# Sparse attention with a MoE projection: TensorE transposes for the first keys and queries, whole w_out tiles, and a planner that models a shared port

## The chip, the cores and the metric

The kernel runs on one core of one Trainium2 chip. The metric is the device time of one execution in microseconds, the median of several runs. Engines are named as in the profile: PE is TensorE (PEld its weight loads), DVE is VectorE, ACT is ScalarE, POOL is GpSimd, SP is SyncE, which here only issues DMAs. PSUM is the accumulator memory that PE writes, SBUF the working memory.

## The reference

Four batches of eight heads, 768 positions, head size 64. Scores are masked by blocks of 32: a block pair is kept if it is within one of the diagonal, in the first or last block row or column, or among three sampled blocks per row. The softmax times v, gathered over heads, gives x (3072 tokens by 512). A two-layer projection with a per-unit leaky slope follows.

```python
scores = scale * np.matmul(q, k.transpose(0, 1, 3, 2))
mask = np.abs(blk_i - blk_j) <= window          # or first/last block, or sampled
scores = np.where(mask, scores, -1000000000.0)
attn = softmax(scores)                          # max, exp, sum + 1e-9
x = (attn @ v).transpose(0, 2, 1, 3).reshape(B * S, H * D)
h = x @ w_in                                    # 512 -> 2048
g = np.maximum(h, 0.0) + alpha * np.minimum(h, 0.0)
out = g @ w_out                                 # 2048 -> 512
```

## The kernel before

**Precision.** All inputs are f32. Each matmul operand is split into two f16 tiles, a high half and a low half (value times a power of two, minus the high half), and products are summed from three or four such terms. High halves are made in `times` (L325 on ACT, L327 on DVE, L329 on POOL), low halves in `rest` (L333 on DVE in one two-input instruction, or L335 and L336 on POOL in a multiply and a subtraction).

**Attention.** Twelve chunks: each batch has three chunks of two 128-row query tiles. A unit is one chunk and one pair of heads (48 units), a step is one head's query tile in a unit (192 steps, 16 a chunk). A step is: scores on PE (L498, high and low query halves in one 128-deep operand against the key tile `kt` and against `ks`, which is `kt` with its two 64-partition halves swapped), bias and minimum on DVE (L508), exp with row sum on ACT (L515), a scale (L519) and reciprocal (L523), high and low half of the probabilities `ph`, one DMA transpose of `ph` into `pt` on SP's queue (L538). After the four steps of a unit PE multiplies by v (`av`, L552), and ACT and DVE write the two halves of `x` (L563, L568).

**Keys and queries.** `prep_k` loads two heads of keys, takes a sum of squares on ACT, a norm through PE and a scale on DVE, makes `kn` with both halves, transposes it by DMA into `kt` (`emit_k_t`, L444) and copies that by two DMAs into `ks` (`emit_k_swap`, issued in the helper `load`, L364). `prep_q` does the same for queries and transposes `qn` into `qt` (`emit_q_t`, L410). All these DMAs are issued on SP's queue.

**Weights.** w_in tiles (16, each 128x1024 int32 words as loaded) are staged in the memory of `wo`; w_out tiles are loaded as two halves of 128x512 words, one in a buffer of the tag `vf` (shared with the raw keys and values), one in a buffer of the tag `g` (shared with the MoE's activations). Three integer operations turn the words into scaled f32: n1 (L708, DVE), n2 (L713 on ACT or L715 on DVE), n3 (L720, DVE). Then come a sum of squares, a scale, and high and low halves. For w_in the low half comes from PE (L776, L777, copied by L781).

**MoE.** For each chunk, eight groups j of two 128-wide slices of the hidden layer: up projection on PE (L852), activation on DVE (L862, L863), high half on ACT (L868), low half on POOL (L873), down projection on PE (L891). The first up projection of a chunk needs the chunk's four `x`; the first down projection needs w_out's halves, whose scale needs all 16 w_out tiles.

**The planner.** The class `Plan` decides the order of all work and, where there is a choice (`alts`), the engine. Every operation has a priority in units of attention steps, a cost per engine, dependences and buffers that it takes and frees. `Plan.run` simulates the engines in time with these costs and starts, whenever an engine is free, the ready operation of lowest priority number. The order that comes out is fixed for each engine: on the chip each engine runs its list in that order and waits where an input is late. Two costs for DVE stand for POOL idle and POOL busy:

```python
MOE_LAG = 11.753          # steps between a chunk's last step and its MoE
MAX4 = {"DVE": (0.55, 1.1), "ACT": 0.85}     # a 128x768 high half
LOW4 = {"DVE": (0.94, 1.5), "POOL": 2.8}     # a 128x768 low half
```

`V_WI + W_WI * f` and `V_WO + W_WO * f` are the priorities of weight tile f. The pools `o` and `s` are two PSUM buffers each, `a` and `h` one each.

Of the kernel before, what the change touches and what calls it, by code (L numbers as in the profile page):

```python
# [54 lines left out]
class Plan:  # L55
# [5 lines left out]
    LAT = {"PE": 0.15, "DVE": 0.11, "ACT": 0.12, "POOL": 0.08}  # L61
# [4 lines left out]
    def buf(self, pool):  # L66
        return Buf(pool)
# [105 lines left out]
def attn_moe(ctx: ExitStack, tc: tile.TileContext, q, k, v, sampled, w_in, w_out, alpha, out):  # L173
# [100 lines left out]
    bias = cpool.tile([P, NT, S], BF16, name="bias")  # L274
    nident = cpool.tile([P, P], F16, name="nident")
# [64 lines left out]
    MAX4 = {"DVE": (0.55, 1.1), "ACT": 0.85}  # L340
    LOW4 = {"DVE": (0.94, 1.5), "POOL": 2.8}
# [668 lines left out]
```

## Time and profile before

| | us |
|---|---|
| median of 3 runs | 908.3 (907.07 to 909.03) |
| the profiled execution | 911.63 |
| its span | 909.9 |
| PE busy | 802.7 (88%) |
| DVE busy | 714.8 (79%) |
| ACT busy | 553.3 (61%) |
| POOL busy | 505.2 (56%) |
| mean granted TensorE clock | 0.955 |

Busy times are sums of instructions over the span. The page also cuts the span into 40 slices of 22.7 us and gives the busy share of each in tenths. A group of instructions has one line: its place in the kernel, engine, operation, output and inputs by name, count, busy time, mean in ns, and the idle time of its engine just before, with what ended most of that. A minimum, median and maximum stand in the view by tile or line. The stretches that the prediction shows list the busy time of each engine in a part of the span, the granted clock (1 is full speed) and the share of time in which the 16 DMA engines were busy, which can come out a little above 1.

### The profile page before, as it was taken

The page shows a single profiled execution, that of the slowest core. Times are in us where ns is not written, and L with a number is a line of the kernel's source. Part 1 is how long each engine was busy: PE and PEld are TensorE (multiplying, and loading weights), DVE is VectorE, ACT ScalarE, POOL GpSimd, SP SyncE. Part 2 cuts the span into 40 slices and gives each one's busy share as a digit, 9 for nine tenths or more (in the row PEclk, how much of TensorE's full clock was granted, in tenths as well). Part 3 has the DMA queues.
Part 4 walks back from the last instruction along what each step waited for, and adds up shares of the span by engine and source line. Part 5 has one row for each costly group of instructions (what it writes and reads, how often), then busy time and mean ns, then how long its engine had stood idle before and what let it go on. Part 6 is the DMA issues. An engine that isn't in the chain of part 4 may idle for free.

```text
span 909.9 us, 16946 instructions
## 1 busy us (share of the span) xinstructions
PE 802.7 (88%) x6089; PEld 528.9 (58%) x6089; DVE 714.8 (79%) x1468; ACT 553.3 (61%) x1185; POOL 505.2 (56%) x413
## 2 busy tenths in 40 slices
PE   3757438988888999999989999999989999999998
PEld 1323215646555766666656766566656667666664
DVE  4899999997888898879987877688987887765232
ACT  6697667875755756757566565666566556664111
POOL 3154445775656667566576665456567566555221
PEclk9867767999999999999999999999999999999999
DMA  9997986988997876969976868969976868655000
GB/s 264 288 263 180 203 210 117 185 134 136 170 175 133 156 138 129 210 130 189 202 154 128 128 128 150 189 119 193 187 140 118 156 117 139 116 117 105 1 24 23
DMA packets 393236, 137.45 MB, mean 151 GB/s; under 512 B 355236, under 2 KB 383936, under 8 KB 393152
## 3 DMA queue, kind: packets, MB, share of 16 engines
q1 hardware_dynamic: 354816, 94.41, 60.2%
q10 hardware_dynamic: 38272, 41.95, 16.8%
q8 instruction: 47, 0.77, 0.3%
q14 instruction: 37, 0.30, 0.1%
q0 software_dynamic: 64, 0.02, 0.0%
HBM read 35.67 MB, written 6.29 MB: 46 GB/s over the span
## 4 chain that ended last, share of the span: by engine, by line
DVE 33%; PE 29%; issue 13%; ACT 12%; DMA 5%; POOL 4%; ACTq 2%; POOLq 0%; DVEq 0%
PE h L852 11%; PE o L891 10%; DVE e L508 6%; ACT e L515 5%; PE sp L498 4%; DVE g L862 4%; DVE ph L333 3%; PE av L552 3%; DVE ph L327 3%; ACT ph L325 2%; DVE g L863 2%; ACTq L364 2%; DMA kf<-in_k_dram 2%; DVE wo L720 2%; DVE qn L403 2%
## 5 line engine op out<-in xcount | busy, mean ns | idle before, releaser
L852 PE MATMUL h<-x,wi 128*128 128x256 f16 x2304 | 270.3, 274 | 14.9 <-DVE g L863 14.7
L852 PEld LDWEIGHTS <-wi 128*128 128x128 f16 x2304 | 227.1, 99 | 57.0 <-issue 18.4
L515 ACT ACTIVATE e<-e,nm 128x768 f32<-128x768 f32 x192 | 178.6, 930 | 114.4 <-DVE nm L508 106.7
L891 PE MATMUL o<-wo,gh 128*128 128x512 f16 x768 | 230.8, 382 | 0.0
L336 POOL TENSOR_TENSOR ph<-e,ph 128x768 f16<-128x768 f32 x128 | 216.7, 1693 | 10.7
L873 POOL TENSOR_TENSOR gl<-g,gh 128x512 f16<-128x512 f32 x96 | 119.1, 1241 | 177.8 <-ACT gh L868 173.4
L335 POOL TENSOR_SCALAR e<-e,rs 128x768 f32<-128x768 f32 x128 | 130.2, 1017 | 157.3 <-DVE ph L327 81.2
L508 DVE CUSTOM_DVE_ANT_0 e<-sp,bias,cs 128x768 f32<-128x768 f32 x192 | 191.9, 1008 | 17.0 <-PE sp L498 10.2
L891 PE MATMUL o<-wo,gl 128*128 128x512 f16 x384 | 146.4, 381 | 1.8 <-POOL gl L873 1.8
L868 ACT CAST gh<-g 128x512 f16<-128x512 f32 x96 | 59.1, 616 | 135.4 <-DVE g L863 120.1
L498 PE MATMUL sp<-kt,qt 128*128 128x512 f16 (+1 forms) x384 | 99.1, 341 | 46.7 <-DVE nm L508 46.5
L498 PEld LDWEIGHTS <-qt 128*128 128x128 f16 x768 | 74.4, 101 | 111.3 <-issue 58.4
L325 ACT ACTIVATE ph<-e,rs 128x768 f16<-128x768 f32 x114 | 105.8, 928 | 28.1 <-DVE rs L523 21.5
L891 PEld LDWEIGHTS <-gh 128*128 128x128 f16 x768 | 74.9, 99 | 80.0 <-issue 3.4
L862 DVE TENSOR_SCALAR g<-h,am 128x256 f32<-128x256 f32 x192 | 83.2, 474 | 48.3 <-PE h L852 46.7
L552 PE MATMUL av<-pt,v 128*64 128x256 f16 x1728 | 108.0, 281 | 1.8 <-DMA pt<-ph 1.5
L552 PEld LDWEIGHTS <-v 128*64 128x64 f16 x1728 | 93.6, 113 | 18.8 <-issue 14.7
L498 PE MATMUL sp<-ks,qt 128*128 128x512 f16 (+1 forms) x384 | 99.3, 342 | 0.0
L523 DVE RECIPROCAL rs<-dn 128x1 f32<-128x1 f32 x192 | 29.0, 156 | 76.0 <-ACT dn L519 75.1
L333 DVE SCALAR_TENSOR_TENSOR ph<-e,rs,ph 128x768 f16<-128x768 f32 x64 | 75.2, 1175 | 9.9 <-ACT ph L325 8.6
L863 DVE SCALAR_TENSOR_TENSOR g<-h,gsc,g 128x512 f32<-128x512 f32 x96 | 72.1, 751 | 3.4
L891 PEld LDWEIGHTS <-gl 128*128 128x128 f16 x384 | 37.8, 99 | 49.4 <-POOL gl L873 3.8
(119 smaller groups left out, 734.1 us busy)
## 6 DMA issues: line engine op xcount, KB each, us to landing
wo<-in_moe_w_in_dram ACTq DMA_DIRECT2D x16, 512.0 KB, 6.7
raw<-in_moe_w_out_dram ACTq DMA_DIRECT2D x32, 256.0 KB, 3.8
kf<-in_k_dram ACTq DMA_DIRECT2D x16, 384.0 KB, 4.1
qf<-in_q_dram ACTq DMA_DIRECT2D x48, 128.0 KB, 4.1
ks<-kt SPq DMA_DIRECT2D x32, 192.0 KB, 4.3
vf<-in_v_dram ACTq DMA_DIRECT2D x16, 384.0 KB, 7.6
out_dram<-ob ACTq DMA_DIRECT2D x24, 256.0 KB, 3.5
pt<-ph SPq DMA_TRANSPOSE x192, 4.1
```

The lines of the kernel that those rows point to most:

```text
L325: nc.scalar.activation(dst, src, AF.Copy, scale=scale)
L333: nc.vector.scalar_tensor_tensor(dst, src, scale, hi, ALU.mult, ALU.subtract)
L335: nc.gpsimd.tensor_scalar(tmp, src, scale, 1.0, ALU.mult, ALU.mult)
L336: nc.gpsimd.tensor_tensor(dst, tmp, hi, ALU.subtract)
L498: nc.tensor.matmul(T["sp", n][:, a:z], T["qt", u][:, h, i, :], kt[:, h, a:z], start=(x == 0), stop=(x == 1))
L508: nc.vector.tensor_tensor_reduce(T["e", n], T["sp", n], bias[:, t0 + j % w, :], scale=T["cs", c][:, hp : hp + 1], scalar=3.0e38, op0=ALU.a ...
L515: nc.scalar.activation(T["e", n], T["e", n], AF.Exp, bias=T["nm", n], scale=-1.0, accum_out=T["su", n])
L552: nc.tensor.matmul(av[h * D : (h + 1) * D, : n * P], v2[:, h, t, vv, :], T["pt", u, h][:, pl * NT + t, :], start=(m == 0), stop=(m == len( ...
L852: nc.tensor.matmul(ph[:, i, :], win(w, f, ct), x[:, ct, :], start=(m == 0), stop=(m == len(terms) - 1))
L862: nc.vector.tensor_scalar(g[:, i, :], ph[:, i, :], 0.0, am1[:, f : f + 1], ALU.min, ALU.mult)
L873: nc.gpsimd.tensor_tensor(T["gl", c, j], T["g", c, j], T["gh", c, j], ALU.subtract)
L891: nc.tensor.matmul(T["o", c][t], g[:, i, t * P : (t + 1) * P], wout(w, f), start=(f == 0 and m == 0), stop=(f == NF - 1 and m == 2),)
```

## The change

There are four parts. First, for batch 0 the key tiles `kt` and `ks`, and for chunk 0 the query tiles `qt`, are no longer transposed by DMA: PE transposes the f16 halves into a PSUM buffer of the pool `o` (128x128 blocks for `kt` and `qt`; 128x64 blocks written to the opposite partition half for `ks`, so that no swap copy is needed), and ACT or DVE copies the result to SBUF. Second, w_out tiles are loaded whole (128x1024 words) into two new buffers `wr` or into the two buffers of `x`, the MoE's input, whichever is free. Third, the planner's cost model: latencies and a slack factor per engine are larger, DMAs are 15% longer, and operations whose cost is a pair take part in a port: a DVE operation with a pair starts only when no POOL operation is in its locked part (the second number of POOL's pair), and a POOL operation with no unlocked part waits for DVE. POOL may now also make the 128x768 high halves. Fourth, buffer counts and the priority constants are new. The path for probabilities by PE (`P_PE`, `emit_p_pe`, `emit_p_copy`) is written but off, since `P_PE` is 0.

```diff
-MOE_LAG = 11.753
-MOE_BOOST = 7.325
-V_WI = -10.661
-W_WI = 1.102
-V_WO = 12.217
-W_WO = 1.038
+MOE_LAG = 7.669
+MOE_BOOST = 7.439
+V_WI = -2.266
+W_WI = 0.799
+V_WO = -2.974
+W_WO = 1.152
...
-PL_V = -12.594
-P_V = -6.546
+PL_V = -35.527
+P_V = 5.696
-LD = 4
+LD = 5
+P_PE = 0
+RAWP = ["wr", "x"]
+K_PE = 1
+BUFS = {"wr": 2, "vf": 4, "qf": 4, "qt": 3, "qn": 2, "ph": 4, "e": 4, "pt": 4, "x": 2, "g": 3, "junk": 2, "sid": 2, "kt": 4, "ks": 4, "v2": 4, "gh": 3, "gl": 3}
...
-    LAT = {"PE": 0.15, "DVE": 0.11, "ACT": 0.12, "POOL": 0.08}
+    LAT = {"PE": 0.2, "DVE": 0.2, "ACT": 0.2, "POOL": 0.15}
+    SLACK = {"PE": 1.0, "DVE": 1.08, "ACT": 1.05, "POOL": 1.1, "SP": 1.0}
...
         def cost(o, e):
             c = o.alts[e]
-            if isinstance(c, tuple):
-                c = c[1] if idle["POOL"] > now + 0.2 else c[0]
-            return c
+            return self.SLACK[e] * (sum(c) if isinstance(c, tuple) else c)
+
+        def hold(o, e):
+            c = o.alts[e]
+            if not isinstance(c, tuple):
+                return 0.0
+            if e == "DVE":
+                return max(port["to"] - now, 0.0) if port["from"] <= now else 0.0
+            return max(port["dve"] - now, 0.0) if c[0] == 0 else 0.0
...
-                    best = min(o.alts, key=lambda e: max(idle[e] - now, 0.0) + load[e] + cost(o, e))
+                    best = min(o.alts, key=lambda e: max(idle[e] - now, hold(o, e)) + load[e] + cost(o, e))
+                    if hold(o, best) > 1e-9:
+                        continue
...
+                    if isinstance(o.alts[best], tuple):
+                        if best == "DVE":
+                            port["dve"] = now + c
+                        else:
+                            port["from"], port["to"] = now + self.SLACK[best] * o.alts[best][0], now + c
...
-                    rings["SP" if o.eng == "SP" else "ACT"].append([o.dma, o])
+                    rings["SP" if o.eng == "SP" else "ACT"].append([1.15 * o.dma, o])
...
-    bufs = dict(kt=5, ks=5, v2=5, vf=5, qf=6, qt=3, qn=2, ph=4, e=3, pt=3, x=2, g=3, gh=3, gl=3, junk=2, sid=2)
+    bufs = dict(BUFS)
...
-    MAX4 = {"DVE": (0.55, 1.1), "ACT": 0.85}
-    LOW4 = {"DVE": (0.94, 1.5), "POOL": 2.8}
+    MAX4 = {"DVE": (0.55, 0), "ACT": 0.85, "POOL": 1.05}
+    LOW4 = {"DVE": (0.94, 0), "POOL": (1.05, 1.65)}
...
+    def emit_k_pe(b, hp, x, h):
+        nat = T["kn", b, hp]
+        key = ("kt", "ks")[x]
+        if (key, b, hp) not in T:
+            T[key, b, hp] = wt(key, [P, 2, NT, P], F16)
+        t = T["kp", b, hp, x, h] = ps_o.tile([P, 2 * DM], F16, tag="o", name="kp")
+        for i in range(NT):
+            g = h * NT + i
+            if x == 0:
+                nc.tensor.transpose(t[:, i * P : (i + 1) * P], nat[:, g].rearrange("p a d -> p (a d)"), ident16)
+                continue
+            for a in range(2):
+                nc.tensor.transpose(t[D * (1 - a) : D * (2 - a), i * P : (i + 1) * P], nat[:, g, a, :], ident16)
...
+    def emit_q_pe(u):
+        n = chunks[units[u][0]][2]
+        T["qt", u] = wt("qt", [P, 2, n, P], F16)
+        T["qp", u] = ps_o.tile([P, 2 * DM], F16, tag="o", name="qp")
+        for g in range(2 * n):
+            nc.tensor.transpose(T["qp", u][:, g * P : (g + 1) * P], T["qn", u][:, g].rearrange("p a d -> p (a d)"), ident16)
...
+        if b == 0 and K_PE:
+            for x, d, kb in ((0, o_kt, kbuf), (1, o_ks, ksbuf)):
+                d[b, hp] = []
+                for h in range(2):
+                    tb = plan.buf("o")
+                    t = plan.op(prio - 2, {"PE": 0.4 + 0.4 * x}, lambda x=x, h=h: emit_k_pe(b, hp, x, h), [o], [tb, kb[b, hp]], [nb])
+                    d[b, hp].append(plan.op(prio - 2, {"ACT": 0.85, "DVE": 0.9}, lambda e, x=x, h=h: emit_k_copy(e, b, hp, x, h), [t], [kb[b, hp]], [tb]))
+            return
...
-        if h == 0:
-            t = wt("vf", [P, 512], I32, "raw")
-        else:
-            t = wt("g", [P, 512], I32, "raw")
-        load(e, t, wo_src[:, f, h * 512 : (h + 1) * 512])
+        t = wt(h.pool, [P, 1024], I32, "raw")
+        load(e, t, wo_src[:, f, :])
...
-        for h in range(2):
-            rb = plan.buf("vf" if h == 0 else "g")
-            o = plan.op(p - 8 + 0.1 * h, LQ, lambda e, f=f, h=h: emit_load_w(e, "wo", f, h), [n3wi[min(NF - 1, 8 + f // 2)]], [rb, plan.buf("ld")], dma=0.8)
-            o = plan.op(p, {"DVE": (0.22, 0.6)}, lambda f=f, h=h: emit_n1("wo", f, h), [o] + free, [], [rb])
-            o = plan.op(p, {"ACT": 0.7, "DVE": (0.34, 0.5)}, lambda e, f=f, h=h: emit_n2(e, "wo", f, h), [o], [], [rb])
-            n3.append(plan.op(p, {"DVE": (0.34, 0.5)}, lambda f=f, h=h: emit_n3("wo", f, h), [o], [], [rb]))
+        rb = plan.buf(*RAWP)
+        o = plan.op(p - 8, LQ, lambda e, f=f, rb=rb: emit_load_w(e, "wo", f, rb), [n3wi[min(NF - 1, 8 + f // 2)]], [rb, plan.buf("ld")], dma=1.6)
+        o = plan.op(p, {"DVE": (0.36, 0)}, lambda f=f: emit_n1("wo", f, 0), [o] + free, [], [rb])
+        o = plan.op(p, {"ACT": 1.27, "DVE": (0.6, 0)}, lambda e, f=f: emit_n2(e, "wo", f, 0), [o], [], [rb])
+        n3 = [plan.op(p, {"DVE": (0.61, 0)}, lambda f=f: emit_n3("wo", f, 0), [o], [], [rb])]
...
-                gl[j] = plan.op(p - MOE_BOOST, {"POOL": 0.2 + 1.1 * f}, lambda j=j: emit_gl(c, j), [o], [lbs[j]], [gb[j], hbs[j]])
+                gl[j] = plan.op(p - MOE_BOOST, {"POOL": (0, 0.1 + 1.08 * f)}, lambda j=j: emit_gl(c, j), [o], [lbs[j]], [gb[j], hbs[j]])
```

The copies of the transposed keys and queries (`emit_k_copy`, `emit_q_copy`) are one ACT or DVE copy of 128x768 or 128x512 f16 elements from PSUM.

More of the change, by code (lines that the diff above doesn't have):

```diff
@@ L93, in run @@
         order = []
+        port = {"from": 0.0, "to": 0.0, "dve": 0.0}
         busy = dict.fromkeys(self.ENGINES, 0.0)
@@ L133, in run @@
                     for b in o.alloc:
-                        self.free[b.pool] -= not b.live
+                        if not b.live:
+                            b.pool = next(x for x in b.pools if self.free[x] > 0)
+                            self.free[b.pool] -= 1
                         b.live = True
@@ L540, in emit_p_t, with emit_p_pe, emit_p_copy @@
         )
+    def emit_p_pe(n, x):
+        u, j = steps[n]
+        w = chunks[units[u][0]][2]
+        h, i = divmod(j, w)
+        if ("pt", u, h) not in T:
+            T["pt", u, h] = wt("pt", [P, 2 * NT, w * P], F16)
+        t = T["tp", n, x] = ps_o.tile([P, 2 * DM], F16, tag="o", name="tp")
+        for g in range(NT):
+            nc.tensor.transpose(t[:, g * P : (g + 1) * P], T["ph", n][:, x, g * P : (g + 1) * P], ident16)
+    def emit_p_copy(e, n, x):
+        u, j = steps[n]
+        w = chunks[units[u][0]][2]
+        h, i = divmod(j, w)
+        dst = T["pt", u, h][:, x * NT : (x + 1) * NT, i * P : (i + 1) * P]
+        src = T["tp", n, x][:, :S].rearrange("p (x j) -> p x j", j=P)
+        if e == "ACT":
+            nc.scalar.copy(dst, src)
+        else:
+            nc.vector.tensor_copy(dst, src)
     def emit_av(u):
@@ L663, in values @@
         p = first[u + 1] + 2
-        last = [o_pt[n] for n in range(first[u], first[u + 1])]
-        o = plan.op(p - 2, {"PE": 0.4 + 1.92 * f}, lambda: emit_av(u), last + [o_v2[b, hp]],
+        last = [x for n in range(first[u], first[u + 1]) for x in o_pt[n]]
+        o = plan.op(p - 2, {"PE": 0.3 + 1.88 * f}, lambda: emit_av(u), last + [o_v2[b, hp]],
                     [ab, xbuf[c]], [ptbuf[u, 0], ptbuf[u, 1], vbuf[b, hp]])
@@ L811, in attn_moe @@
             for x in (f - 1, f):
-                o = plan.op(p + 0.1, {"ACT": 0.63, "DVE": (0.36, 0.7), "POOL": 0.82}, lambda e, x=x: emit_w_hi(e, "wi", x), [gs[-1], prev])
+                o = plan.op(p + 0.1, {"ACT": 0.63, "DVE": (0.36, 0), "POOL": 0.82}, lambda e, x=x: emit_w_hi(e, "wi", x), [gs[-1], prev])
                 if WI_LO == "pe":
@@ L817, in attn_moe @@
                 else:
[L818 removed]
+                    prev = o_wi[x] = plan.op(p, {"DVE": (0.67, 0), "POOL": (0.8, 1.25)}, lambda e, x=x: emit_w_lo(e, "wi", x), [o], [], [sb])
     o_gsc = plan.op(V_WI + W_WI * NF - 2, {"DVE": 0.5}, emit_gsc, gs + [o_al])
```

73 lines of the change are left out of this document (49 added, 24 removed).

## The prediction

> **What bounds the kernel now.** I first read the page's busy shares and its forty slices.
>
> ```profile
> PE 802.7 (88%) x6089; PEld 528.9 (58%) x6089; DVE 714.8 (79%) x1468; ACT 553.3 (61%) x1185; POOL 505.2 (56%) x413
> PE   3757438988888999999989999999989999999998
> DVE  4899999997888898879987877688987887765232
> ```
>
> No single engine bounds the whole span. From slice 10 on PE is full; before it DVE is full and PE is not. So I cut the span where the first MoE product starts and asked for busy times by stretch, with two later stretches that hold a change of batch.
>
> ```profile
> 0.00:42.00 42.00, 21.46 (x56) 10.62 (x57) 28.62 (x85) 27.04 (x59) 10.73 (x27) 0.94 1.04 270
> 42.00:147.00 105.00, 58.59 (x292) 30.31 (x290) 96.97 (x214) 79.81 (x184) 49.87 (x39) 0.70 0.86 206
> 147.00:207.00 60.00, 55.56 (x424) 37.31 (x423) 58.89 (x113) 45.82 (x97) 42.59 (x33) 0.95 0.89 155
> 207.00:300.00 93.00, 80.69 (x650) 53.36 (x648) 75.86 (x151) 55.63 (x118) 56.82 (x46) 0.98 0.88 156
> 400.00:500.00 100.00, 94.54 (x738) 63.55 (x735) 85.54 (x177) 64.20 (x133) 61.26 (x48) 0.98 0.82 160
> 600.00:700.00 100.00, 92.22 (x728) 62.01 (x728) 85.06 (x173) 65.04 (x133) 62.85 (x48) 1.00 0.88 159
> ```
>
> After the stretch's length the columns are PE, PEld, DVE, ACT and POOL busy, granted clock, DMA share, GB/s. Up to 147 us PE works 21.46 + 58.59 = 80.0 us and DVE 28.62 + 96.97 = 125.6 us; DVE has 8.0 us of gaps in the 105 us of the second stretch. Behind 147 us PE works 802.7 - 80.0 = 722.7 us in the 762.9 us that are left, so it idles 40 us there, 12.3 + 5.5 + 7.8 = 25.6 us of it in the three stretches with a batch change. The end is therefore: the time until the first up projection may start, then 722.7 us of PE work, then 40 us of gaps. Most of the edits act on the first term, so the next view is what lets that projection start: two rows in order of time, and the rows of the w_out tiles with minimum, median and maximum in ns, and the first and last start.
>
> ```profile
> 146.79 3.46 PE L852 MATMUL h<-x,wi 128*128 128x256 f16 x16
> 147.48 0.41 DVE L568 SCALAR_TENSOR_TENSOR x<-av,x 128x256 f16<-128x256 f32 x1
> L720 DVE SCALAR_TENSOR_TENSOR wo<-raw,wo x32: 396/414/1871, 75.6 to 147.9; 128x256 int32<-128x256 int32 x32
> L708 DVE TENSOR_SCALAR wo<-raw x32: 269/280/1726, 74.0 to 142.1; 128x256 int32<-128x256 int32 x32
> L715 DVE SCALAR_TENSOR_TENSOR wo<-raw,wo x17: 403/412/1054, 74.4 to 146.7; 128x256 int32<-128x256 int32 x17
> ```
>
> The fourth x of chunk 0 ends within a microsecond of the first up projection, and the conversion of w_out ends with it (75.6 to 147.9): attention of chunk 0 and both weight conversions share DVE and finish together. What DVE has done by then, by line (busy us, mean ns):
>
> ```profile
> L720 DVE SCALAR_TENSOR_TENSOR wo<-raw,wo 128x256 int32<-128x256 int32 x31 | 23.0, 762 | 1.5 <-ACT raw L713 1.3
> L508 DVE CUSTOM_DVE_ANT_0 e<-sp,bias,cs 128x768 f32<-128x768 f32 x22 | 21.9, 1006 | 3.5 <-PE sp L498 3.5
> L720 DVE SCALAR_TENSOR_TENSOR wi<-wo,wi 128x512 int32<-128x512 int32 x16 | 12.5, 786 | 0.2 <-ACT wo L713 0.2
> L708 DVE TENSOR_SCALAR wo<-raw 128x256 int32<-128x256 int32 x32 | 11.1, 377 | 0.0
> L715 DVE SCALAR_TENSOR_TENSOR wi<-wo,wi 128x512 int32<-128x512 int32 x13 | 8.8, 679 | 0.1
> L715 DVE SCALAR_TENSOR_TENSOR wo<-raw,wo 128x256 int32<-128x256 int32 x17 | 8.0, 486 | 0.0
> L327 DVE TENSOR_SCALAR ph<-e,rs 128x768 f16<-128x768 f32 x8 | 7.6, 953 | 0.0
> L333 DVE SCALAR_TENSOR_TENSOR ph<-e,rs,ph 128x768 f16<-128x768 f32 x6 | 6.6, 1102 | 0.0
> L708 DVE TENSOR_SCALAR wi<-wo 128x512 int32<-128x512 int32 x16 | 6.6, 423 | 0.0
> L523 DVE RECIPROCAL rs<-dn 128x1 f32<-128x1 f32 x20 | 2.9, 153 | 2.7 <-ACT dn L519 2.6
> ```
>
> The means lie far above the medians of the view before (762 against 414 ns). The order of time shows why: a DVE instruction beside a two-input POOL subtraction lasts as long as that does.
>
> ```profile
> 99.13 1.76 POOL L336 TENSOR_TENSOR ph<-e,ph 128x768 f16<-128x768 f32 x1
> 99.31 1.73 DVE L708 TENSOR_SCALAR wo<-raw 128x256 int32<-128x256 int32 x1
> ```
>
> That is 1.73 us for work with a median of 0.28, while L508, which reads its scores from PSUM, keeps its 1.006 us.
>
> **The change, part by part.**
>
> *w_out tiles whole.* 32 half conversions become 16 whole ones. Now they cost 23.0 + 11.1 + 8.0 = 42.1 us of DVE by 147 us. The same three instructions on whole tiles stand in the w_in rows: 16 x 0.786 + 16 x 0.423 + 8.5 x 0.679 = 25.1 us (8.5 is half of 17, the share that DVE takes from ACT). That saves 17.0 us, if whole w_out tiles meet POOL as seldom as w_in's do. The other bound is merging alone, no stall avoided: 32 x 0.414 + 32 x 0.280 + 17 x 0.412 = 29.2 us by the medians, less 16 x 0.68 + 16 x 0.423 + 8.5 x 0.679 = 23.4 us whole (0.68 for L720 too, which has L715's shape): 5.8 us. I take the middle, **11.4 us**, since DVE meets POOL per instruction and there are half as many, but more attention will run beside them.
>
> *The plan knows the port.* It no longer starts such a DVE operation while POOL subtracts, and picks another. It also slows every cost by up to a tenth and lets POOL take the 128x768 high halves. What can go in the front, beside w_out: 8 x (0.953 - 0.62) = 2.7 us on L327, 0.62 being this line's median over the span (row below); 6 x 0.1 = 0.6 us on L333, if 1.0 is its undisturbed time; 16 x (0.786 - 0.68) = 1.7 us on L720 of w_in. So 0 to 5.0 us. The plan's times will drift from the chip's, so half: **2.5 us**.
>
> ```profile
> L327 DVE TENSOR_SCALAR ph<-e,rs x78: 600/620/1993, 55.3 to 827.7; 128x768 f16<-128x768 f32 x78
> 52.51 2.36 POOL L335 TENSOR_SCALAR e<-e,rs 128x768 f32<-128x768 f32 x1 [1.92 <-ACT ph L325]
> 50.03 4.15 DVE L333 SCALAR_TENSOR_TENSOR v<-vf,sv,v 128x768 f16<-128x768 f32 x4
> ```
>
> The lower two rows speak for the half: POOL's one-input multiply, which the new plan lets run beside DVE (its 1.05 of LOW4), took 2.36 us beside DVE's two-input operations. The Trainium skill ("SBUF — State Buffer", SBUF: two separate sides) says the same as a rule: the shared port pair is an exclusive lock for a whole instruction, against any GpSimd operation, so a plan that exempts L335 still has stalls in it. By that rule this term would be nearer 0 than 5.0, and the sum 2.5 us smaller.
>
> *Keys and queries by TensorE.* Gone are four key transposes, four query transposes and eight swap copies, all on SP's queue and in the first 60 us:
>
> ```profile
> 25.57 9.95 SPq L444 DMA_TRANSPOSE kt<-kn  x2
> 42.52 0.85 PE L498 MATMUL sp<-kt,qt 128*128 128x512 f16 x2
> q1 hardware_dynamic: 10496, 3.67, 32.1%
> kt<-kn SPq DMA_TRANSPOSE x4, 9.4
> L308 ACT ACTIVATE bias<-mkr 128x768 bf16<-128x768 f32 x6 | 4.6, 805 | 1.1 <-PE mkr L293 1.1
> L781 ACT CAST wi<-d 128x512 f16<-128x512 f32 x16 | 9.4, 587 | 4.0 <-PE d L777 4.0
> ```
>
> A key transpose takes 9.4 us to land here, its issue holds SP's queue, and the first score waits until 42.5 us. q1's 32.1% of 62 us is 20 us of all sixteen DMA engines at a time when they are full (share 1.04 up to 42 us), so the weight and value loads gain too. In its place: 4 x (12 + 24) + 16 = 160 PE transposes and 20 evictions. No row shows a transpose of this kind; between the mean weight load of the first stretch (10.62/57 = 0.19 us) and the mean score matmul (0.85/2 = 0.43 us, with two to four times the columns) they take 30 to 68 us of PE; I take 30, the narrower tile being nearer, all of it before the first up projection, where PE idles 147 - 80.0 = 67 us: nothing on the path. Without that gap it would be 30 us. The evictions read PSUM like L308 and L781: 16 x 0.805 + 4 x 0.587 = 15.2 us, on ACT, which idles 42 - 27.04 = 15.0 us in the first stretch. All of it on DVE would be some 19 us (16 x 1.006 + 4 x 0.7); none, 0. With ACT the cheaper and freer, a third on DVE: **5 us lost**. The scores can start near 20 us. DVE is the bound, so the 22 us are not won; what is won is DVE idleness, 13.4 us up to 42 us, of which 10.4 less 0.2 come before the first statistic (row below), plus 3.5 us waiting for scores (L508's row): 0 to 7, I take **4 us**.
>
> ```profile
> 10.41 0.15 DVE L313 TENSOR_SCALAR uq<-ssq 128x1 int32<-128x1 int32 x1 [3.74 <-ACT junk L321]
> ```
>
> *New constants.* w_out's conversion gets priorities -3 to 14 where it had 12 to 28, w_in's ends at 10, MOE_LAG falls from 11.8 to 7.7 steps. By the first up projection 22 steps had been scored where chunk 0 has 16; a step costs DVE 1.006 + 0.153 + (7.6 + 6.6)/20 = 1.87 us. Between 0 and 6 of them can come later (11.2 us); I take 3: **5.6 us** earlier. Their matmuls come later too: two pairs a step of 0.85 us each at the lower clock of the front, some 0.8 of that at full clock, 3 x 2 x 0.68 = **4.1 us** given back.
>
> *Buffers.* e and pt get a fourth tile each; kt, ks, v2 and vf lose their fifth, qf two. Behind 207 us PE waits for DVE, in all 22.9 us:
>
> ```profile
> PE h L852 <- DVE g L863: 13.5, 11, 2.5
> PE sp L498 <- DVE nm L508: 9.4, 10, 3.5
> ```
>
> A better order with more e and pt can take away up to 15 us; later key tiles can add as much. I take **6 us** off.
>
> *Sum.* 11.4 + 2.5 + 4 + 5.6 - 5 = 18.5 us earlier, less 4.1, plus 6: 20.4 us. The profiled execution's span of 909.9 becomes 889.5; its time lay 1.7 us above its span (911.6) and 3.3 above the median of the runs (908.3), so the forecast is 889.5 + 1.7 - 3.3 = **888 us**.
>
> **The rivals.**
>
> *More than the front.* Stalls are in every stretch: L327 has 78 instructions up to 1.99 us. If the new order also closes most of the 40 us behind 147 us (25 instead of 6) and the w_out term reaches 17, the gain is 20.4 + 19 + 5.6 = 45 us: 863. For it: DVE holds 85 of 100 us between 400 and 500, so stalls there can still reach PE. Against: PE is 92 to 96% busy in those stretches, so each has little left to give.
>
> *The front moves and nothing follows.* Evictions wholly on DVE (19 instead of 5) and only the 5.7 us of merging: 20.4 - 14 - 5.6 = 0.8, and -5.2 with no gain behind: 908 to 914. The change then does what it says and is hidden by the DVE bound. That the port bookkeeping does nothing is in here.
>
> *Slower: batch changes lose their cover.* With four key tiles the next batch's first can only be written when the last chunk's first unit has been scored, 12 steps before the batch ends. Of 192 steps 170 follow the first up projection, to 831 us, 4.0 us each (row below), so batches change near 251, 443 and 635 us and 12 steps are 48 us of notice, against a chain of load, square, scale, high, low, transpose and swap. MOE_LAG's cover falls from 11.8 x 4.0 = 47 to 31 us. For it: the three stretches with a batch change already hold 25.6 us of PE idleness.
>
> ```profile
> L508 DVE CUSTOM_DVE_ANT_0 e<-sp,bias,cs x192: 991/1008/1019, 44.0 to 831.2; 128x768 f32<-128x768 f32 x192
> 215.75 9.33 DMA kf<-in_k_dram
> ```
>
> Against: this load, a piece of that chain and of the chain of waits, is 9.3 us, far below 48. If it decides, from a delay of over 31 us on, 15 us more are lost at each of three changes: 45 - 20 = +25, some 933; at 10 us each, 918.
>
> **How the numbers follow.** The forecast has 0.58, more than the front 0.18, nothing follows 0.09, batch changes 0.15. Changes within 0.2% (2 us) can't be told from none. Of "nothing follows" 0.05 lies within that, 0.01 below and 0.03 above. Faster 0.77, same 0.05, slower 0.18. The forecast's own range, from its bounds short of all meeting at one end, is 872 to 904; the range out to the rivals is 860 to 914, which leaves out the far side of the batch changes and the tail of the second case.
>
> **What would show it.** Right: first score near 20 us; first up projection near 128 us instead of 146.8; w_out's L720 x16 at a mean under 0.85 us; ks and kt copies from SP only 24 and 12; PE idleness behind the first up projection at or below 40 us. Evictions mainly on ACT. Wrong: a first up projection at 145 us or later; DVE rows still twice their medians; PE waits growing in the stretches of the batch changes.

## The result, and the profile after

The changed kernel takes **878.3 us** (median of four runs, 876.9 to 880.1) beside 907.7 us of the kernel before on the same chip: a ratio of 0.968, 95% interval 0.965 to 0.971. 888 had been forecast, with a range of 860 to 914. The sign and the range held; the split of the gain did not, as the profile shows at once. First its page (in the changed kernel's line numbers L947 is the up projection, L986 the down projection, L558 the scores, L568 the bias, L358 and L359 POOL's low half, L356 DVE's low half, L350 and L352 the high half on DVE and POOL, and L805, L812 and L817 the three conversion steps n1, n2, n3 of the weights):

```profile
span 876.4 us, 17097 instructions
PE 802.7 (92%) x6249; PEld 533.7 (61%) x6249; DVE 672.0 (77%) x1395; ACT 554.9 (63%) x1188; POOL 560.4 (64%) x458
PE   3856476999999999999999999999999999999997
DVE  3889989999977778779877777788787787666322
```

PE's busy time is the same 802.7 us as before, with 160 instructions more; its idle time fell from 909.9 - 802.7 = 107.2 to 73.7 us. Where, is read from the stretches before and behind the first up projection, first of the changed kernel, then of the kernel before (columns as in the prediction: PE, PEld, DVE, ACT and POOL busy, clock, DMA share, GB/s):

```profile
0.00:152.20 152.20, 91.55 (x511) 48.46 (x512) 128.03 (x275) 107.61 (x240) 86.96 (x84) 0.78 0.77 194
152.20:876.40 724.20, 711.17 (x5740) 485.21 (x5738) 544.02 (x1121) 447.29 (x949) 473.44 (x375) 1.00 0.79 144
```

```profile
0.00:146.80 146.80, 79.85 (x346) 40.79 (x347) 125.39 (x299) 106.72 (x242) 60.60 (x66) 0.77 0.91 225
146.80:909.90 763.10, 722.81 (x5745) 488.13 (x5743) 589.40 (x1171) 446.57 (x944) 444.58 (x347) 0.99 0.75 137
```

The first up projection starts at 152.2 us, **5.4 us later** than before, not 18.5 earlier. Behind it PE's gaps shrank from 763.1 - 722.8 = 40.3 to 724.2 - 711.2 = **13.0 us**, and PE's own work there from 722.8 to 711.2 us. So 5.4 - 27.3 - 11.6 = -33.5 us of span: all of the gain, and more, lies behind the point that the prediction tried to move. (The profiled execution of the kernel before took 911.6 us, 3.9 above its median, so the two profiles lie 33.5 us apart where the medians lie 29.4 apart.) PE's two main waits for DVE in that part, first before and then after, shrank from 27.2 to 7.9 us:

```profile
PE h L852 <- DVE g L863: 14.7, 13, 2.5
PE sp L498 <- DVE nm L508: 12.5, 13, 3.5
```

```profile
PE h L947 <- DVE g L958: 7.3, 9, 2.1
PE sp L558 <- DVE nm L568: 0.6, 3, 0.2
```

Each row gives the total, the number of waits and the longest. The three stretches with a batch change, 87, 95 and 92% busy before, are full now:

```profile
207.00:300.00 93.00, 91.17 (x743) 62.54 (x740) 76.47 (x164) 57.81 (x123) 59.26 (x47) 1.00 0.88 165
400.00:500.00 100.00, 98.44 (x794) 67.04 (x793) 81.41 (x174) 68.80 (x143) 69.86 (x54) 1.00 0.90 167
600.00:700.00 100.00, 99.08 (x798) 67.46 (x797) 77.76 (x169) 68.65 (x149) 69.97 (x55) 1.00 0.90 168
```

DVE behind the first up projection fell from 589.4 to 544.0 us. The groups of the changed kernel that show how, and the parts that replaced others in the front:

```profile
L356 DVE SCALAR_TENSOR_TENSOR ph<-e,rs,ph 128x768 f16<-128x768 f32 x64 | 76.6, 1197 | 11.1 <-ACT ph L348 10.6
L350 DVE TENSOR_SCALAR ph<-e,rs 128x768 f16<-128x768 f32 x44 | 41.8, 950 | 3.5 <-DMA pt<-ph 2.8
L352 POOL TENSOR_SCALAR ph<-e,rs 128x768 f16<-128x768 f32 x38 | 45.1, 1186 | 30.5 <-DVE rs L583 21.7 <-DVE wi L817 4.6 <-DMA pt<-ph 2.5
L817 DVE SCALAR_TENSOR_TENSOR wo<-raw,wo 128x512 int32<-128x512 int32 x16 | 15.8, 988 | 0.0
L817 DVE SCALAR_TENSOR_TENSOR wi<-wo,wi 128x512 int32<-128x512 int32 x16 | 13.1, 817 | 0.8 <-ACT wo L810 0.8
L812 DVE SCALAR_TENSOR_TENSOR wo<-raw,wo 128x512 int32<-128x512 int32 x14 | 10.4, 744 | 0.0
L805 DVE TENSOR_SCALAR wo<-raw 128x512 int32<-128x512 int32 x16 | 9.5, 602 | 0.0
L805 DVE TENSOR_SCALAR wi<-wo 128x512 int32<-128x512 int32 x16 | 9.4, 599 | 0.0
L812 DVE SCALAR_TENSOR_TENSOR wi<-wo,wi 128x512 int32<-128x512 int32 x11 | 9.1, 832 | 0.0
L483 PE MATMUL kp<-ident,kn 128*64 128x128 f16 x96 | 5.3, 267 | 1.8 <-ACT kt L489 1.0 <-DVE kt L491 0.7
L480 PE MATMUL kp<-ident,kn 128*128 128x128 f16 x48 | 5.2, 272 | 3.7 <-DVE uq L336 2.5 <-ACT ks L489 0.7 <-DVE ks L491 0.5
L489 ACT COPY kt<-kp 128x768 f16<-128x768 f16 x5 | 4.0, 796 | 3.5 <-PE kp L480 2.8 <-DVE qt L506 0.5 <-issue 0.2
```

DVE's high halves of probabilities went from 78 to 44 instructions, 64.3 to 41.8 us; 38 are on POOL. It also made ten high halves of v before (12.0 us) and makes none now. The means of the two `ph` rows did not fall (1175 to 1197 ns, 827 to 950). The w_out conversion costs 15.8 + 10.4 + 9.5 = 35.7 us where it cost 42.1, but w_in's went up from 12.5 + 8.8 + 6.6 = 27.9 to 13.1 + 9.1 + 9.4 = 31.6 us.

### The profile page after: what moved, and what is told of

Same layout as the page of the kernel before. It is cut to its first block, busy times and chain, and to the rows that moved or that the text cites. A ratio compares the mean times of both kernels' runs of the same rounds, so it can differ in the third digit from the quotient of the medians.

```text
span 876.4 us, 17097 instructions
## 1 busy us (share of the span) xinstructions
PE 802.7 (92%) x6249; PEld 533.7 (61%) x6249; DVE 672.0 (77%) x1395; ACT 554.9 (63%) x1188; POOL 560.4 (64%) x458
## 3 DMA queue, kind: packets, MB, share of 16 engines
q10 hardware_dynamic: 35968, 41.95, 16.7%
## 4 chain that ended last, share of the span: by engine, by line
PE 63%; DVE 14%; issue 8%; POOL 6%; ACT 6%; ACTq 2%; DMA 1%; POOLq 0%; DVEq 0%
PE h L947 21%; PE o L986 21%; PE sp L558 10%; PE av L633 8%; DVE e L568 2%; ACT e L575 2%; POOL ph L359 2%; ACTq L387 2%; POOL gl L968 2%; DVE wo L817 1%; DVE g L957 1%; POOL e L358 1%; ACT ph L348 1%; DVE g L958 1%; DVE qn L426 1%
## 5 line engine op out<-in xcount | busy, mean ns | idle before, releaser
L947 PE MATMUL h<-x,wi 128*128 128x256 f16 x2304 | 267.2, 273 | 7.3 <-DVE g L958 7.3
L947 PEld LDWEIGHTS <-wi 128*128 128x128 f16 x2304 | 225.0, 98 | 47.9 <-issue 10.2
L986 PE MATMUL o<-wo,gh 128*128 128x512 f16 x768 | 228.5, 379 | 0.0
L359 POOL TENSOR_TENSOR ph<-e,ph 128x768 f16<-128x768 f32 x128 | 217.9, 1702 | 10.7
L568 DVE CUSTOM_DVE_ANT_0 e<-sp,bias,cs 128x768 f32<-128x768 f32 x192 | 192.0, 1007 | 26.2 <-PE sp L558 16.6
L358 POOL TENSOR_SCALAR e<-e,rs 128x768 f32<-128x768 f32 x128 | 132.0, 1032 | 110.4 <-ACT ph L348 60.4
L986 PE MATMUL o<-wo,gl 128*128 128x512 f16 x384 | 145.5, 379 | 0.6 <-POOL gl L968 0.6
L558 PEld LDWEIGHTS <-qt 128*128 128x128 f16 x768 | 74.2, 102 | 84.9 <-issue 32.1
L986 PEld LDWEIGHTS <-gh 128*128 128x128 f16 x768 | 74.7, 98 | 78.6 <-issue 0.8
L558 PE MATMUL sp<-kt,qt 128*128 128x512 f16 (+1 forms) x384 | 98.9, 341 | 21.6 <-DVE nm L568 19.4
L348 ACT ACTIVATE ph<-e,rs 128x768 f16<-128x768 f32 x110 | 101.6, 926 | 12.3 <-DVE rs L583 5.8
L633 PE MATMUL av<-pt,v 128*64 128x256 f16 x1728 | 105.9, 278 | 0.0
L558 PE MATMUL sp<-ks,qt 128*128 128x512 f16 (+1 forms) x384 | 98.4, 339 | 0.0
L356 DVE SCALAR_TENSOR_TENSOR ph<-e,rs,ph 128x768 f16<-128x768 f32 x64 | 76.6, 1197 | 11.1 <-ACT ph L348 10.6
L986 PEld LDWEIGHTS <-gl 128*128 128x128 f16 x384 | 37.6, 98 | 46.3 <-POOL gl L968 1.1
L352 POOL TENSOR_SCALAR ph<-e,rs 128x768 f16<-128x768 f32 x38 | 45.1, 1186 | 30.5 <-DVE rs L583 21.7
## 6 DMA issues: line engine op xcount, KB each, us to landing
qf<-in_q_dram ACTq DMA_DIRECT2D x48, 128.0 KB, 4.3
```

The lines of the kernel that those rows point to most:

```text
L348: nc.scalar.activation(dst, src, AF.Copy, scale=scale)
L358: nc.gpsimd.tensor_scalar(tmp, src, scale, 1.0, ALU.mult, ALU.mult)
L359: nc.gpsimd.tensor_tensor(dst, tmp, hi, ALU.subtract)
L558: nc.tensor.matmul(T["sp", n][:, a:z], T["qt", u][:, h, i, :], kt[:, h, a:z], start=(x == 0), stop=(x == 1))
L568: nc.vector.tensor_tensor_reduce(T["e", n], T["sp", n], bias[:, t0 + j % w, :], scale=T["cs", c][:, hp : hp + 1], scalar=3.0e38, op0=ALU.a ...
L633: nc.tensor.matmul(av[h * D : (h + 1) * D, : n * P], v2[:, h, t, vv, :], T["pt", u, h][:, pl * NT + t, :], start=(m == 0), stop=(m == len( ...
```

## The experiments

In most of them one part is undone in the changed kernel; in three a part is put into the kernel before. When the first up projection starts, DVE has done the scores of 22 or 23 steps, so its start can be compared between kernels; only e4 (20 steps) and e12 (21) start it with less attention done, and so look earlier than they are. The table gives the ratio to the kernel before on the same chip (95% interval), and from each profile the first up projection, PE's idle time ahead of it, and the gaps and PE's work behind it. The profile is one execution, up to 4 us from the median.

| kernel | us | ratio | first up | idle ahead | gaps behind | work behind |
|---|---|---|---|---|---|---|
| before | 907.7 | 1 | 146.8 | 67.0 | 40.3 | 722.8 |
| changed | 878.3 | 0.968 (0.965-0.971) | 152.2 | 60.7 | 13.0 | 711.2 |
| e1, keys by DMA | 892.3 | 0.985 (0.981-0.988) | 164.8 | 80.7 | 14.6 | 715.2 |
| e2, no port in the plan | 928.1 | 1.025 (1.022-1.028) | 168.9 | 72.0 | 35.9 | 722.2 |
| e3, three e and pt | 915.0 | 1.010 (1.007-1.014) | 153.9 | 63.9 | 35.6 | 723.8 |
| e4, w_out halves | 889.3 | 0.982 (0.979-0.985) | 149.6 | 60.1 | 21.4 | 718.3 |
| e5, MOE_LAG 7.9 | 878.4 | 0.969 (0.965-0.972) | 151.8 | 60.0 | 13.3 | 711.3 |
| e6, W_WI 0.82 | 884.2 | 0.975 (0.972-0.978) | 151.8 | 58.8 | 15.7 | 714.5 |
| e7, old constants | 889.1 | 0.979 (0.975-0.984) | 158.0 | 66.8 | 15.8 | 714.3 |
| e8, before + tiles | 917.8 | 1.012 (1.008-1.016) | 133.5 | 56.8 | 55.1 | 726.2 |
| e9, before + port plan | 908.2 | 1.000 (0.998-1.003) | 173.4 | 92.9 | 18.3 | 712.9 |
| e10, e9 + tiles | 895.7 | 0.987 (0.981-0.994) | 162.6 | 86.9 | 18.4 | 710.5 |
| e11, no high half on POOL | 880.9 | 0.969 (0.964-0.975) | 144.8 | 57.1 | 18.8 | 715.0 |
| e12, other constants | 883.1 | 0.972 (0.968-0.976) | 147.9 | 60.1 | 17.3 | 718.5 |

### e1: first keys and queries by DMA again

```diff
-K_PE = 1
+K_PE = 0
```

> The changed kernel (878.3 us) with the first keys and queries transposed by DMA again, all else as it is. The changed kernel's first up projection starts at 152.2 us, later than the 146.8 us of the kernel before, so the prediction's term (earlier first product) did not come. Theory A, the gain lies behind the first up projection (gaps 13.0 us there instead of 40.4): first scores move back from 24.5 to some 42 us, about 12.5 us of PE transposes and 4.7 us of DVE copies go away, the first up projection stays within 5 us of 152 and the time within 5 us of 878. Theory B, the early scores carry the gain: the first up projection moves to 165 us or later and the time to 890 or more.

```profile
0.00:164.80 164.80, 84.08 (x346) 42.49 (x347) 127.63 (x273) 106.28 (x235) 75.37 (x77) 0.77 0.85 198
164.80:894.60 729.80, 715.24 (x5744) 487.16 (x5742) 542.79 (x1119) 442.44 (x945) 472.39 (x374) 1.00 0.77 144
```

892.3 us, 14 us more than the changed kernel. Theory B was right for this part: the first up projection moves 12.6 us back, to 164.8 (165 or later had been named), and the gaps behind it hardly change (14.6 against 13.0). TensorE's transposes are worth their 14 us ahead of the first up projection, while DVE's work there is the same (127.6 against 128.0, with one step and the 4.7 us of copies fewer): it is its idle time, 37.2 against 24.2 us, that they take away.

### e2: the port taken out of the plan

```diff
         def hold(o, e):
-            c = o.alts[e]
-            if not isinstance(c, tuple):
+            if True:
                 return 0.0
```

> The changed kernel with the port taken out of the plan: no operation is held back for it, costs as in the changed kernel (slack, latencies), so DVE operations cost their undisturbed time whatever POOL does. Theory A, the port in the plan closes the gaps behind the first up projection: PE's gaps there grow from 13 to 25 us or more, the slow DVE rows (low halves, high halves) get longer means, time 890 or more. Rival, the plan's port moves stalls but saves none (w_in's conversion rows got slower in the changed kernel, 27.9 to 31.6 us): time within 5 us of 878.

```profile
168.90:927.00 758.10, 722.18 (x5740) 488.69 (x5738) 612.35 (x1165) 397.13 (x880) 472.63 (x369) 0.99 0.75 137
```

928.1 us, slower than the kernel before. Gaps behind the first up projection are 35.9 us, and that projection starts 16.7 us later. The groups of DVE show both ways in which the port acts:

```profile
L356 DVE SCALAR_TENSOR_TENSOR ph<-e,rs,ph 128x768 f16<-128x768 f32 x64 | 91.0, 1422 | 5.8 <-ACT ph L348 4.1 <-POOL ph L352 0.4
L350 DVE TENSOR_SCALAR ph<-e,rs 128x768 f16<-128x768 f32 x88 | 80.4, 915 | 1.6
```

Low halves take 1422 instead of 1197 ns (more stalls), and DVE gets 88 high halves instead of 44, since a plan without the port counts them at the undisturbed cost whatever POOL does. DVE is busy for 762 instead of 672 us. The rival (stalls are only moved) falls. The plan of the kernel before knew POOL roughly, by its two costs, so this run is not the kernel before with the other parts added.

### e3: three tiles of e and pt

```diff
-BUFS = {... "e": 4, "pt": 4, ...}
+BUFS = {... "e": 3, "pt": 3, ...}
```

> The changed kernel with three tiles of e and of pt, as before, instead of four. If the fourth tiles close the gaps behind the first up projection: PE gaps there grow by 10 us or more and the time is 888 or more. If the order of the plan does it: within 5 us of 878.

915.0 us. The first up projection is where it was (153.9), and behind it the gaps are 35.6 us: nearly all of the improvement there is gone. What DVE waits for, in e3 and in the changed kernel:

```profile
DVE e L568 <- POOL ph L359: 14.5, 16, 2.5
DVE e L568 <- PE sp L558: 12.6, 17, 1.3
```

```profile
DVE e L568 <- PE sp L558: 16.6, 26, 1.5
DVE e L568 <- POOL gl L968: 5.2, 6, 1.3
DVE e L568 <- POOL ph L359: 4.0, 6, 0.7
```

L568 writes a tile of e; with three of them it waits 14.5 us, 16 times, for POOL to have finished a low half and given its tile back; with four, 4.0 us. In the kernel before, also with three tiles, it waited less:

```profile
DVE e L508 <- POOL ph L336: 6.6, 7, 1.2
```

That this wait is what opens PE's gaps is not shown by e3 alone; the next kernels bear on it.

### e8: the new buffer counts in the kernel before

```diff
-    bufs = dict(kt=5, ks=5, v2=5, vf=5, qf=6, qt=3, qn=2, ph=4, e=3, pt=3, ...)
+    bufs = dict(kt=4, ks=4, v2=4, vf=4, qf=4, qt=3, qn=2, ph=4, e=4, pt=4, ...)
```

> The kernel before with four tiles of e and pt (three before), four of kt, ks, v2, vf and qf (five, five, five, five and six before), nothing else. If the fourth tiles by themselves close gaps behind the first up projection: gaps there 40 to some 18 us, time 880 to 895. If they only serve a plan that knows the port and was fitted to them: 900 to 915, gaps at 35 us or more.

```profile
0.00:133.50 133.50, 76.75 (x346) 39.01 (x347) 112.75 (x265) 96.49 (x218) 59.87 (x66) 0.81 0.96 229
133.50:914.80 781.30, 726.15 (x5746) 490.14 (x5744) 603.33 (x1203) 463.20 (x973) 442.07 (x341) 0.98 0.73 137
```

917.8 us, 1.2% slower than the kernel before. Its first up projection starts 13.3 us **earlier**, almost what the prediction wanted, and its gaps behind grow by 14.8 us, to 55.1: the time won ahead is lost behind. It is lost at once:

```profile
133.50:207.00 73.50, 54.48 (x398) 35.52 (x397) 67.44 (x136) 47.69 (x102) 37.90 (x30) 0.83 0.76 150
```

Up to 207 us PE idles 19.0 us here, against 4.4 in the kernel before, and from there on the two have the same gaps (36.1 and 35.9). The first activation of the MoE (`g`) starts at 158.1 us here and at 151.2 before, so an early first up projection did not mean that the MoE could run on. L508 waits only 0.8 us for POOL's low half (6.6 before), so free tiles of e do not help where the order around them is the old one. It also takes away fifth tiles of kt, ks, v2 and vf and two of qf, in a kernel whose w_out halves still borrow vf; which of these costs it was not separated.

### e9 and e10: the new planner in the kernel before, without and with the buffers

```diff
 # in the changed kernel: K_PE = 0, w_out in halves, the eight old priority constants, LD = 4, and
-BUFS = {"wr": 2, "vf": 4, "qf": 4, ... "e": 4, "pt": 4, ... "kt": 4, "ks": 4, "v2": 4, ...}
+BUFS = {"wr": 2, "vf": 5, "qf": 6, ... "e": 3, "pt": 3, ... "kt": 5, "ks": 5, "v2": 5, ...}   # e9 only
```

> The kernel before with only the changed planner (port, slack, latencies, DMA times, the costs of pairs, POOL for high halves); first keys by DMA, w_out in halves, old constants, old buffers with three e and three pt. Undoing the port in the changed kernel cost 50 us and undoing the fourth tiles 37. If the port in the plan is worth its gain alone: 870 to 890, gaps behind the first up projection under 25 us. If it needs the fourth tiles to have other work to put beside POOL: 900 to 920, gaps of 30 us or more, though DVE's busy time falls by 25 us or more from 714.8.

> The same with the buffers of the changed kernel too (four e, four pt, four kt, ks, v2, vf, qf): port and tiles together, without TensorE transposes, whole w_out tiles and new constants. If port and tiles together make the gain behind the first up projection: gaps there under 20 us, and the time 885 to 900, the rest up to 878 being the first keys, the w_out tiles and the constants (14, 11 and 11 us by the runs that undid them, which cannot all add up). If all parts are needed together: 905 or more.

e9 and e10, each the stretch behind its first up projection:

```profile
173.40:904.60 731.20, 712.88 (x5744) 485.45 (x5742) 533.97 (x1107) 450.40 (x953) 476.33 (x373) 1.00 0.79 143
```

```profile
162.60:891.50 728.90, 710.46 (x5740) 485.22 (x5738) 551.32 (x1127) 443.31 (x942) 468.26 (x368) 1.00 0.78 143
```

e9 ends where the kernel before ends (ratio 1.000), but neither theory described how: the gaps behind fall to 18.3 us as the first said, PE's work there falls to 712.9 us, and all of it is paid for ahead, where the first up projection moves to 173.4 us, 26.6 later. DVE falls by 40.9 us to 673.9. Ahead of the first up projection it is busy for 14.5 us more, and 16 high and low halves of w_out, 13.9 us, now stand there, where the kernel before has none (its first starts at 157.4 us):

```profile
L356 DVE SCALAR_TENSOR_TENSOR wo<-wo,s_wo 128x512 f16<-128x512 f32 x9 | 8.6, 956 | 0.7 <-POOL wo L352 0.5
L350 DVE TENSOR_SCALAR wo<-wo,s_wo 128x512 f16<-128x512 f32 x7 | 5.3, 757 | 0.2
```

```profile
L333 DVE SCALAR_TENSOR_TENSOR wo<-wo,s_wo x15: 740/1185/2127, 157.4 to 204.2; 128x512 f16<-128x512 f32 x15
```

So the smaller gaps behind may in part be DVE work moved ahead; how much of the 22.0 us that is, was not separated. The row of e3 is there again, and mostly gone with the fourth tiles (e9, then e10):

```profile
DVE e L568 <- POOL ph L359: 18.2, 22, 1.9
```

```profile
DVE e L568 <- POOL ph L359: 6.6, 4, 2.4
```

This wait does not by itself make PE idle: e9 has more of it than e3 (18.2 against 14.5 us), and half of e3's gaps. With the tiles (e10) the first up projection comes 10.8 us earlier and the time is 895.7 us, as the second theory had it, but the gaps behind stay (18.4). In e3 the same tiles counted behind, 22.6 us of gaps, and not ahead; why was not found. So in the kernel before the tiles alone lose 1.2%, the port alone changes nothing, and both together gain 1.3%.

### e4 and e7: w_out in halves, and the old constants

```diff
 # e4
-        rb = plan.buf(*RAWP)
-        n3 = [...one whole tile...]
+        for h in range(2):
+            rb = plan.buf("vf" if h == 0 else "g")
+            ...n1, n2, n3 on 128x256 words, costs (0.22, 0), 0.7 or (0.34, 0), (0.34, 0)
 # e7
-MOE_LAG, MOE_BOOST, V_WI, W_WI, V_WO, W_WO, PL_V, P_V = 7.669, 7.439, -2.266, 0.799, -2.974, 1.152, -35.527, 5.696
+MOE_LAG, MOE_BOOST, V_WI, W_WI, V_WO, W_WO, PL_V, P_V = 11.753, 7.325, -10.661, 1.102, 12.217, 1.038, -12.594, -6.546
```

> The changed kernel with w_out loaded and converted in halves again, in buffers of the raw values and of the activations. By the DVE rows whole tiles cost 15.8 + 10.4 + 9.5 = 35.7 us against 42.1 in halves, so 6.4 us of DVE in the front: theory A (front not decisive) time 878 to 884; theory B (each us of DVE in the front is a us of the end) 884 to 890; if the borrowed buffers hold up values and activations as well, over 890.

> The changed kernel with all eight priority constants of the kernel before (MOE_LAG, MOE_BOOST, V_WI, W_WI, V_WO, W_WO, PL_V, P_V). The prediction gave them 5.6 us less 4.1. Theory, constants matter only with the rest: w_out's conversion runs late again, first up projection between 140 and 160 us, gaps behind it 13 to 30 us, time 885 to 900. Rival, the constants carry most of the gain: 905 or more. Rival, they are worth nothing: 874 to 883.

```profile
149.60:889.30 739.70, 718.26 (x5752) 488.24 (x5750) 563.15 (x1139) 452.31 (x966) 483.12 (x381) 0.99 0.76 143
```

e4: 889.3 us, 11 more than the changed kernel, at the upper end of theory B's band. The first up projection is 2.6 us earlier (149.6), but with three steps fewer scored, 5.6 us of DVE work at the prediction's 1.87 us each, so B's reason is neither shown nor refuted: what was won ahead by leaving steps for later is lost in the gaps behind (21.4) and PE's work there (718.3). e7: 889.1 us, in the first theory's band; here the first up projection is 5.8 us later.

### e5 and e6: two controls

```diff
-MOE_LAG = 7.669    # e5
+MOE_LAG = 7.9
-W_WI = 0.799       # e6
+W_WI = 0.82
```

> A control: the changed kernel with MOE_LAG 7.9 in place of 7.669, a nudge of a quarter step that reshuffles the order and takes nothing away. If the kernel's constants are fitted so closely to its own plan that any change of the plan loses, this loses 10 us or more as well, and the losses of the runs that undid a part (14, 50, 37 and 11 us) are partly that. If the parts themselves count: within 6 us of 878.3.

> A second control: the changed kernel with W_WI 0.82 in place of 0.799, so w_in's tile 15 has its priority a third of a step later. As for the other control: within 6 us of 878.3 if the parts count, 888 or more if the fit of the constants counts.

e5 did not reshuffle anything: every engine's list came out in the same order as in the changed kernel, so it is a repeat of it on another chip, and gives 878.4 us. e6 has another order and takes 884.2 us: 6 us (0.7%) is what this one nudge of a fitted constant costs. Against that measure the 50, 37 and 14 us of e2, e3 and e1 stand; of the 11 us of e4 and of e7 about half may be no more than a plan that isn't fitted to them.

### e11: no high half on POOL

```diff
-    MAX4 = {"DVE": (0.55, 0), "ACT": 0.85, "POOL": 1.05}
+    MAX4 = {"DVE": (0.55, 0), "ACT": 0.85}
```

> The changed kernel without POOL as a choice for the 128x768 high halves (38 of 192 probabilities went there). If the choice of engine makes part of the port plan's gain (DVE took 88 high halves without the port, 44 with it): DVE's busy time rises by 10 us or more, time 884 to 895. If the order alone makes it: within 4 us of 878.

880.9 us: by its ratio (0.964 to 0.975) not to be told from the changed kernel. DVE takes 69 high halves instead of 44 and is busy for 680.3 us, 8 more, and the first up projection is 7.4 us earlier with 5.8 us more of gaps behind. POOL's high halves are not what makes the gain. DVE's busy time is still 34.4 us below that of the kernel before; what is left to explain that is the order and the choice between DVE and ACT that goes with it, which no run here takes apart.

### e12: other constants, and the first two probabilities by TensorE

```diff
-MOE_LAG = 7.669; V_WI = -2.266; W_WI = 0.799; V_WO = -2.974; W_WO = 1.152; PL_V = -35.527; PL = "ggv"; LD = 5; P_PE = 0
+MOE_LAG = 11.207; V_WI = 0.6; W_WI = 0.562; V_WO = -9.43; W_WO = 0.64; PL_V = -26.323; PL = "gvg"; LD = 6; P_PE = 2
```

(MOE_BOOST and P_V moved slightly too: 7.193 and 4.166.)

> A try at a better version: the changed kernel with w_out's conversion earlier and w_in's steeper or flatter (MOE_LAG 11.2, V_WO -9.4, W_WO 0.64, W_WI 0.56), another pattern of low halves, and the first two steps' probabilities transposed by TensorE too. PE has 13 us of gaps left behind the first up projection and some 60 us before it. If the early probabilities and earlier weights shorten the front: first up projection at 145 us or earlier, time 870 to 876. If PE's gaps are only moved: 877 to 884.

883.1 us. The first up projection is 4.3 us earlier, with two steps fewer scored, the gaps 4.3 us longer and PE's work behind 7.3 us longer. No version here beats the changed kernel.

## Why the prediction was right, and where it was wrong

The total was right by luck in part. Of the 20.4 us that had been forecast, 18.5 were to come from an earlier first up projection, 6 from gaps, less 4.1 of PE's work; what came, by the profiles, is 5.4 lost there, 27.3 won in gaps and 11.6 won in PE's work. The first term was 23.9 us too high and the other two 21.3 and 15.7 us too low, and in the sum these errors leave 13.1 us.

**First up projection 18.5 us earlier.** Wrong, and by the prediction's own list ("a first up projection at 145 us or later") the main step. Its model, in which the start is the sum of DVE's work for chunk 0 and both weights, left out what the new plan does to that stretch: e9 shows that the new planner alone starts it 26.6 us later, 173.4 us, with DVE idle for 173.4 - 139.9 = 33.5 us there instead of 21.4, and busy for 14.5 us more, of the size of the w_out halves (13.9 us) that now stand there. The other parts bring it back to 152.2, by 21.2 us; singly they count for more than that (10.8 us for the buffers in e10, 12.6 for TensorE's transposes in e1, 5.8 for the constants in e7), so they do not add up. In the changed kernel too DVE's work ahead did not fall by the 14.5 us that the terms had for it (11.4 + 2.5 + 5.6 - 5): it rose from 125.4 to 128.0 us, and DVE's idle time there from 21.4 to 24.2. Four low halves of w_out are among it that no term had counted:

```profile
L356 DVE SCALAR_TENSOR_TENSOR wo<-wo,s_wo 128x512 f16<-128x512 f32 x4 | 4.8, 1206 | 0.4 <-ACT wo L348 0.4
```

Term by term:

- *w_out whole*, 11.4 us: 6.4 measured. That is near the lower bound of 5.8, which had no avoided stall in it, but for another reason. By the medians the DVE work went only from 28.8 to 27.0 us, because DVE made the second step of 14 tiles of 16, where 8.5 had been assumed (5.5 x 0.744 = 4.1 us); the time above the medians fell from 13.3 to 8.7 us. L817's mean is still 988 ns, its median 680; a mean under 850 had been asked for. A whole tile meets POOL's subtraction as a half does, for instance

```profile
115.59 1.64 POOL L359 TENSOR_TENSOR ph<-e,ph 128x768 f16<-128x768 f32 x1
115.67 2.10 DVE L817 SCALAR_TENSOR_TENSOR wo<-raw,wo 128x512 int32<-128x512 int32 x1
```

- *the port in the front*, 2.5 us: not there; the 13 high and low halves of probabilities on DVE got about 1.3 us cheaper by their means (953 to 822 and 1102 to 1036 ns), but w_in's three rows got 3.7 us longer. The exclusive lock of the Trainium skill ("SBUF — State Buffer", SBUF: two separate sides) pointed the right way: the term was at zero or below. The Trainium skill states it, for a DVE operation with two SBUF inputs, against a GpSimd operation that reads SBUF, so POOL's one-input operations are in it. The trace agrees: a high half on POOL, median 909 ns, takes 3.19 us while DVE goes through two-input operations of w_in and w_out:

```profile
100.53 3.19 POOL L352 TENSOR_SCALAR ph<-e,rs 128x768 f16<-128x768 f32 x1 [4.61 <-DVE wi L817]
101.67 0.68 DVE L812 SCALAR_TENSOR_TENSOR wo<-raw,wo 128x512 int32<-128x512 int32 x1
102.27 0.68 DVE L817 SCALAR_TENSOR_TENSOR wi<-wo,wi 128x512 int32<-128x512 int32 x1
```

- *early scores*, 4 us: undersized, by e1. The first score came at 24.5 us (20 expected, 42.5 before), and without it the start is 12.6 us later.
- *three steps fewer*, 5.6 us less 4.1: none. 23 steps were scored, not 19.
- *evictions on DVE*, 5 us lost: 4.7 (nine of twenty copies), the rest on ACT, as argued. *Transposes on PE*, 30 us in idle time: 5.3 + 5.2 + 2.0 = 12.5, below both bounds. Back to back a group of twelve takes less than twelve single ones: the rows' means are 267 and 272 ns, but 5.3 us for 96 is 55 ns each.

**Gaps behind, 6 us less.** Right in sign, far too small: 27.3 us. The prediction noted that DVE and not PE made PE wait there, and priced it by the listed waits of 22.9 us with a quarter of them closed. e9, the new planner alone, closes 22.0 us of them, at the price of the late start, and e2 brings 22.9 us back by taking the port out of the plan. In the changed kernel the fourth tiles are needed as well: 22.6 us come back without them (e3). The step that failed is the one that put the port plan into the front term and the buffers into the gap term as separate sums: the port plan closes gaps behind the first up projection, and what the buffers do depends on the rest of the plan, as e3, e8 and e10 show.

**PE's work behind, 4.1 us more.** It was 11.6 us less. Of that, 6.6 us are the same instructions taking less time there (h 270.3 to 267.2, o 377.2 to 374.0, av 95.2 to 94.9 us), at a granted clock of 1.00 instead of 0.99 in that stretch. In e3 and e8, with gaps of 36 and 55 us, the clock is 0.98 and the work 723.8 and 726.2 us. Gaps and a lower clock mostly stand together, so that a gap seems to be paid for twice: before, the clock was 0.95 up to 207 us and 0.98 from there to 300, and e8's 0.98 is 0.83 up to 207 us and 1.00 behind it. It is no rule, though: from 600 to 700 us PE was 92% busy before at a clock of 1.00.

**The rivals.** "More than the front" came nearest: it named gaps behind closing by 25 us (27.3 came) and 863 us, but stacked them on a front that did not move. "Batch changes lose their cover" did not happen: those stretches are 98 to 99% busy with four key tiles. "The front moves and nothing follows" is what e8 is, for tiles alone.

**What stays open.** Why the new planner takes up w_out's halves before the first up projection in e9, and where the other 12.1 us of its delay come from (DVE's idle time), was not separated: its constants were fitted to the other plan, and holding DVE operations back, the longer latencies and the slack all changed at once. `LD`, 4 to 5, was never undone alone. And the parts, undone singly, cost 14 + 50 + 37 + 11 + 11 us, four times the gain, so no division of the 29 us among them is to be had; only paths are, such as 908.2 (port), 895.7 (and tiles), 878.3 (and keys, w_out, constants).

## What to carry to other kernels

When a bound changes from one engine to another within a span, don't take the hand-over point as the quantity to shorten: e8 reached it 13 us earlier and ended 12 us later, e9 26.6 us later and ended even. Add up the bounding engine's idle time on both sides of it, and price an edit by what it does to each. A planner that holds an operation back can keep that operation's tiles longer (DVE's wait for a tile of e that POOL still held went from 6.6 us to 18.2 in e9), so a better model of a conflict and one more buffer of what it holds belong in the same trial: apart they were worth 0 and -1.2%, together +1.3%. And before reading small losses of runs that undo a part of a tuned schedule, measure one that only nudges a constant; and compare how much work had been done at the point that is compared.

## What was not expected of the hardware

TensorE transposes of 128x128 f16 blocks in groups of six to twelve ran at about 55 ns each for the 64-wide kind (5.3 us for 96) and 108 ns for the 128-wide kind (5.2 us for 48), between 15 and 38 us, where the mean granted clock was 0.93, and a DVE copy of 128x768 f16 from PSUM took 555 ns, where ACT's took 796:

```profile
L491 DVE COPY kt<-kp 128x768 f16<-128x768 f16 x3 | 1.7, 554 | 0.8 <-PE kp L480 0.8
```

The prediction had priced it by L508's 1.006 us.
